# Moving weight loads and a small filter transpose within the spectral half of a transformer block

## The chip, the cores and the metric

One core of a Trainium2 chip runs the kernel. The metric is the device time of one execution in microseconds; lower is better. Several runs of each kernel are made and their median is given.

## The reference

One block with adaptive layer norm. A vector c makes six rows of 640 scales and shifts; the sequence x (2048 rows of 640, bf16) passes through a spectral filter and then through a gated feed-forward layer.

```python
mod = (silu(c) @ w_mod).reshape(1, 6, 1, -1)
sa, ca, ga, sb, cb, gb = ...                      # six rows of 640
h = layernorm(x) * (1 + ca) + sa
x = x + ga * irfft2(rfft2(h) * (w_r + 1j * w_i))  # filter over sequence and features
h = layernorm(x) * (1 + cb) + sb
x = x + gb * ((silu(h @ w_gate) * (h @ w_up)) @ w_down)
```

The feed-forward width is 1728. All inputs are bf16.

## The kernel before

The order of the work is written out by hand; no scheduler moves anything. Each engine works off its own list in program order, and waits at an instruction until what that instruction needs is there. Loads are issued by SyncE (SP) in program order as well. Eight completion counters are used in turn by the transfers, so a transfer also waits until the one eight before it has landed.

**Spectral part, forward.** Sixteen row tiles are normalised and multiplied with cosine tables (`st_a`, `st_b`, L399 to L419). The result `A_sb` lies in region `rA`. It must then be turned, feature index against time index: for most features by four transposing transfers (`t2_dma`, L537), for the rest on TensorE (`t2_pe`, L556). The filter weights are put together in region `rW` (`turn`, `wsum`).

**Spectral part, filter.** Features are worked in 21 groups of four or fewer. The loop of L770 takes group g through stages which are shifted against each other:

- `stage_a(g + 2)`: `mix` (L574) multiplies the turned features with a small table on TensorE into banks 2 and 3 or 4 and 5, and `prod` (L596) multiplies them with the filter on VectorE.
- `stage_b(g)` (L606): TensorE turns the products, ScalarE copies them. For four groups, 7, 8, 11 and 12 (`PRE`), GpSimd adds the two parts instead and a transposing transfer turns them (`presum`, L617). These are the two turning transfers, one for each pair of groups. Their results are read late, by `stage_c` at g = 14 and g = 20.
- `stage_c(u)` (L633): TensorE applies the small inverse table to two groups at a time into banks 6 and 7 (others near the end); `evac` copies that into `Em` or `Er` in region `rE`.

Into these stages are fitted: the columns of scale and shift (`mod_col`, L591, written into free columns of the bank that `mix` fills, five matmuls of one column for each of five column blocks), the ga row (`ga_mod`), and the special row, frequency zero and Nyquist, which has a small chain of its own (`sp_w`, `sp_wc`, `sp_mm`, `sp_ev`). `sp_w` turns its filter rows by eight tiny transposes into PSUM, `sp_wc` copies them to `Wsp`, and the chain ends in two small transfers into the last partition of `Em` and `Er` (L711, L712).

The block `wm_r` holds four parts of `w_mod`: 0 ga, 1 sb, 2 cb, 3 gb. Parts 0 and 1 are loaded at the start, part 2 ahead of the loop (L553), part 3 in iteration 10 (L792).

**Spectral part, inverse, and second norm.** For 16 tiles, `s1em` and `s1er` (L729, L740) multiply `Em` and `Er`, last partition included, with tables, and L1280 and L1283 finish the tile; VectorE adds the input and writes x1 (L1285). The first two tiles are normalised in iterations 3 and 4, turned by a transposing transfer (`ln2_tr(0)`, L885) and scaled and shifted on GpSimd and ScalarE (`ln2_mod`, L893, L899). The down weights are multiplied by gb on VectorE (`wd_fold`, L923), the first of them in iteration 8.

**Feed-forward part.** The first two tiles take plain products: `gu13` (L1097) for the last 64 columns, then `gu_plain` (L1109) for 13 blocks of gate and up, with silu on ScalarE and a product on VectorE (L1115, L1117), then the down product (L987). The other 14 tiles take products with fewer multiplications (L1139, L1010).

The down weights `Wd_sb` lie in region `rA`, where `A_sb` was. They are loaded after the filter loop (L828 to L833), ahead of the gate and up weights (L836 to L845):

```python
    for h in range(2):
        nc.sync.dma_start(Wd_sb[:, HK * h:HK * h + 6, :],
                          B_w_down[768 * h:768 * h + 768, :].rearrange("(fc fp) d -> fp fc d", fp=P))
    nc.sync.dma_start(Wd_sb[0:RK, 6, :], B_w_down[1536:1632, :])
    nc.sync.dma_start(Wd_sb[0:64, 13, :], B_w_down[1664:1728, :])
    nc.sync.dma_start(Wd_sb[64:RK, 13, :], B_w_down[1632:1664, :])
```

Of the kernel before, what the change touches and what calls it, by code (L numbers as in the profile page):

```python
# [11 lines left out]
BF16 = mybir.dt.bfloat16  # L12
# [6 lines left out]
NT, P = 16, 128  # L19
# [6 lines left out]
RK, HK = 96, 7  # L26
# [134 lines left out]
def _rev(ap, free_off, dims):  # L161
    a = ap[:]
    return bass.AP(tensor=a.tensor, offset=a.offset + free_off, ap=[list(a.ap[0])] + [list(d) for d in dims])
# [3 lines left out]
def adaln_block_kernel(ctx, tc, A_x, A_w_r, A_w_i, B_x, B_w_gate, B_w_up, B_w_down, c, w_mod, out):  # L167
    nc = tc.nc
# [57 lines left out]
    wm_r = rM.cut(12800, [NC5, 4, D])  # L226
# [16 lines left out]
    Wsp = rE.cut(34064, [3, 2, NT, 2], parts=81)  # L243

    psum = ctx.enter_context(tc.tile_pool(name="psum", bufs=1, space=bass.MemoryType.PSUM)).tile([P, 8, 512], F32, name="psum")

    def banks(b, n, shape=None, dt=F32):
        ap = psum[:, b:b + n, :].rearrange("p b e -> p (b e)")
        if dt == BF16:
            ap = ap.bitcast(BF16)  # L250
        if shape is not None:
            ap = ap[:, 0:int(np.prod(shape))]
            if len(shape) > 1:
                ap = ap.rearrange("p (a b) -> p a b", a=shape[0])
        return ap
# [39 lines left out]
    wm_m = wm_v[:, :, 2 * D:6 * D].rearrange("p k (i d) -> p k i d", i=4)  # L295
# [37 lines left out]
    if True:  # L333
# [87 lines left out]
        def wsum(lo, hi, rk, eng):  # L421
            for off in (lo, 161 - hi):
                v = [_rev(Wt, WP * i + 321 * rk + off, [[321, 8], [160, 2], [1, hi - lo]]) for i in range(3)]
                eng.tensor_tensor(v[1], v[2], v[0], ALU.add)  # L424
# [7 lines left out]
                                  sa4[:].unsqueeze(2).unsqueeze(3).to_broadcast([P, 4, 2, 8]))  # L432

        def sp_w():
            tp = psum[0:81, 2, 192:256].bitcast(BF16).rearrange("p (v h a k) -> p v h a k", v=2, h=2, a=2)
            for v in range(2):
                for hl in range(2):
                    for a in range(2):
                        o = 160 * (1 - a if hl else a)
                        nc.tensor.transpose(tp[:, v, hl, a], (Wrev if hl else Wrow)[:, v, o:o + 81], identb[0:16, 0:16])  # L440
            return tp

        def sp_wc(tp):
            for v in range(2):
                nc.vector.tensor_copy(Wsp[:, 2 * v].rearrange("p h k a -> p h a k"), tp[:, v])
            nc.gpsimd.tensor_tensor(Wsp[:, 1], Wsp[:, 0], Wsp[:, 2], ALU.add)

        cps = psum[:, 3, 0:NC5]
# [85 lines left out]
    if True:  # L534
# [15 lines left out]
        t2_dma(3)  # L550
        nc.sync.dma_start(Htab.rearrange("p (t h) v k -> p t h (v k)", h=2)[:, :, 0, :], H_dram.rearrange("p t v k -> p t (v k)"))
        nc.sync.dma_start(RI[:], RI_dram)
        nc.sync.dma_start(wm_r[:, :, 2, :], wm_m[:, :, 2, :])  # L553
        Wd_sb = rA.cut(0, [NFC, D])

        def t2_pe(slot):  # L556
            ls = groups[slot] + (groups[4] if slot == 3 else [])
            n = len(ls)
            tp = banks(slot % 2, 1, [8, 128], BF16)
            for i, l in enumerate(ls):  # L560
                nc.tensor.transpose(tp[:, i, :], A_sb[:, l].rearrange("p t k c r -> p (t k c r)"), identb[:])
            B2 = (rM.cut(38400 + 1024 * slot, [n, 128]) if slot < 2 else rM.cut(10240 + 1024 * (slot - 2), [n, 128]))
            if slot == 0:
                nc.scalar.copy(B2[:, 0:2], tp[:, 0:2, :])
                nc.scalar.copy(B2[:, 2:4], tp[:, 2:4, :])
            else:
                nc.scalar.copy(B2[:], tp[:, :n, :])
            spec.append((B2, 4, slice(ls[0], ls[0] + 4)))
            if n > 4:
                spec.append((B2[:, 4:6], 2, slice(0, 81, 80)))  # L570
            for i, l in enumerate(ls):
                B2of[l] = (B2, i)

        def mix(g):  # L574
            ls = groups[g]
            n = len(ls)
            xps = banks(2 + 2 * (g % 2), 2, [4, 256])
            for i, l in enumerate(ls):
                B2, j = B2of[l][0:2]
                nc.tensor.matmul(xps[:, i, 0:192], lhsT=B2[:, j, :], rhs=KS2, start=True, stop=True)  # L580
                if i == 0:
                    for c5 in {9: (0, 1, 2), 11: (3, 4), 16: (0, 1), 18: (2, 3), 20: (4,)}.get(g, ()):
                        mod_col(psum[:, 2 + 2 * (g % 2), 192 + c5:193 + c5], wm_r[:, :, 2 - g % 2], c5)
            return xps

        def stage_a(g):
            xps = mix(g)
            prod(g, xps, 0)
            prod(g, xps, 1)

        def mod_col(o, w, c5):  # L591
            for k in range(NC5):
                nc.tensor.matmul(o, lhsT=w[:, k, 128 * c5:128 * c5 + 128], rhs=sc_col[:, k:k + 1],
                                 start=(k == 0), stop=(k == NC5 - 1))
# [22 lines left out]
        def presum(g):  # L617
            b, i = PRE.index(g) // 2, 4 * (PRE.index(g) % 2)
            q = Qd[b][:, i:i + 4, :]
            P3 = PPs.pop(g).rearrange("p v h k m l -> p l (v h k m)")  # L620
            nc.gpsimd.tensor_tensor(q, P3[:, :, 0:128], P3[:, :, 64:192], ALU.add)
            Y2s[g] = Yd[b][:, i:i + 4, :]
            if i:
                nc.sync.dma_start_transpose(Yd[b], Qd[b].rearrange("p l j -> p (l j)"))
# [36 lines left out]
        def sp_gather():  # L661
            for B2, n, ls in spec:
                nc.gpsimd.tensor_tensor(B2sp[:, ls], B2[:, 0:n, 127], SA[:, ls], ALU.add)
# [102 lines left out]
        for rk in (0, 8):  # L766
            v = [_rev(Wt, WP * i + 321 * rk + 80, [[321, 8], [160, 2]]) for i in range(3)]
            nc.gpsimd.tensor_tensor(v[1], v[2], v[0], ALU.add)
        sgn_H = Htab.rearrange("p (t h) v k -> p t h (v k)", h=2)
        for g in range(NG + 1):  # L770
            if g == 9:
                nc.gpsimd.tensor_copy(sgnc[:], Kstab[:, 576:577])
            if g == 7:
                sp_gather()
            if 1 < g < NG - 2:
                if g in SPG[1:]:
                    sp_mm(SPG.index(g), g)
                if g == 2:
                    tp = sp_w()
                stage_a(g + 2)  # L780
                if g == 2:
                    wsum(32, 48, 8, nc.gpsimd)
                if g == 3:
                    sp_wc(tp)
                if g in SPG[1:]:
                    sp_ev(SPG.index(g), g)
            if g + 2 in PRE:
                presum(g + 2)
            if g in (4, 9):
                wsum(64, 80, 8 * (4, 9).index(g), nc.gpsimd)  # L790
            if g == 10:
                nc.sync.dma_start(wm_r[:, :, 3, :], wm_m[:, :, 3, :])  # L792
            if g in (11, 12):
                h4 = slice(4 * (g - 11), 4 * (g - 11) + 4)
                nc.gpsimd.tensor_scalar(sgn_H[:, h4, 1], sgn_H[:, h4, 0], sgnc[:, 0:1], 1.0, ALU.mult, ALU.mult)
            if g == 9:
                nc.vector.tensor_copy(modcols[:, 2, :], psum[:, 4, 192:197])
            if g == NG - 3:
                nc.vector.tensor_scalar_add(one_p_cb[:], psum[:, 2, 192:197], 1.0)
            if g in (14, 16):  # L800
                i = 1 - (14, 16).index(g)
                nc.gpsimd.tensor_tensor(RI[:, i], RI[:, i], ga_bc[:], ALU.mult)
            if g < NG and g not in PRE:
                Y2s[g] = stage_b(g, PPs.pop(g))
            if g == SPG[0]:
                sp_mm(0, g)
                sp_ev(0, g)
            if g == 0:
                stage_a(3)
            if g in GAG:  # L810
                ga_mod(320 * GAG.index(g), 0)
            for i in range(2):
                if TUG[i] == g:
                    turn(64, i, (g + 1) % 2, act)
            for u, gs in enumerate(units):
                if CAT[u] == g:
                    stage_c(u)
                    evac(u)
            if g == NG - 1:
                for c5 in range(NC5):  # L820
                    mod_col(psum[:, 3, 192 + c5:193 + c5], wm_r[:, :, 3], c5)
# [3 lines left out]
        s1em(1)  # L825
        gdiag = rL.cut(10496, [NC5, 128])

    for h in range(2):  # L828
        nc.sync.dma_start(Wd_sb[:, HK * h:HK * h + 6, :],
                          B_w_down[768 * h:768 * h + 768, :].rearrange("(fc fp) d -> fp fc d", fp=P))  # L830
    nc.sync.dma_start(Wd_sb[0:RK, 6, :], B_w_down[1536:1632, :])
    nc.sync.dma_start(Wd_sb[0:64, 13, :], B_w_down[1664:1728, :])
    nc.sync.dma_start(Wd_sb[64:RK, 13, :], B_w_down[1632:1664, :])  # L833
    Wgu = rW.cut(0, [2, NC5, 13 * 128])
    Wp13 = const.tile([P, NC5, 128], BF16, name="Wp13")
    nc.sync.dma_start(Wp13[:, :, 0:64], B_w_gate[:, 1664:1728].rearrange("(c5 dp) f -> dp c5 f", dp=P))  # L836
# [581 lines left out]
```

## Time and profile before

| | |
|---|---|
| three runs | 250.68, 253.23, 255.39 us (median 253.23) |
| the profiled execution | 253.03 us, of it a span of 251.3 us from the first to the last instruction |
| mean granted TensorE clock | 0.993 |
| busy share of the span | TensorE 95%, VectorE 81%, ScalarE 67%, GpSimd 31% |
| moved | 31.71 MB, 126 GB/s over the span |
| in time, about | forward to 33 us, filter to 62, inverse to 81, feed-forward from 84 |

All times inside the kernel count from the first instruction of the profiled execution. Lines such as L885 are lines of the kernel before. Engines in the profile: PE is TensorE, PEld its weight loads, DVE VectorE, ACT ScalarE, POOL GpSimd, SP SyncE; a q behind a name stands for that engine's list of issued transfers.

### The profile page before, as it was taken

How to read it: one execution, taken by the hardware profiler on the slowest of the kernel's cores; microseconds unless marked ns; L12 is line 12 of the kernel's file. 1: busy time of each engine (PE TensorE's matmuls, PEld its weight loads, DVE VectorE, ACT ScalarE, POOL GpSimd, SP SyncE). 2: the span in 40 equal slices, each digit the busy share in tenths (PEclk: the TensorE clock that was granted, in tenths of full speed). 3: DMA queues.
4: the chain of work that ended last, by engine and by line, in shares of the span. 5: the costliest groups of instructions: out<-in, count | busy, mean ns of one | idle time of the engine just before them, and what ended most of it. 6: DMA issues, size and time to landing. Idle time of an engine off the chain costs nothing.

```text
span 251.3 us, 5940 instructions
## 1 busy us (share of the span) xinstructions
PE 238.9 (95%) x2230; PEld 186.8 (74%) x2230; DVE 203.8 (81%) x479; ACT 169.3 (67%) x339; POOL 77.0 (31%) x120
## 2 busy tenths in 40 slices
PE   8789998979997899999999999999999999999994
PEld 3578888869997588778887778888765566556773
DVE  3797878967599599689999996878998788779964
ACT  4789887759987297768875387876246777774220
POOL 5368985990420805002002320000442000004410
PEclk9999999999999799999999999999999999999999
DMA  6999969896999999700002320500611000000111
GB/s 210 376 338 301 370 125 188 230 222 199 309 378 281 233 289 154 164 27 4 0 3 56 74 65 18 52 3 3 106 52 55 0 0 1 3 0 1 55 52 52
DMA packets 46254, 31.71 MB, mean 126 GB/s; under 512 B 23985, under 2 KB 43922, under 8 KB 46226
## 3 DMA queue, kind: packets, MB, share of 16 engines
q1 hardware_dynamic: 44288, 26.67, 41.2%
q0 software_dynamic: 1376, 4.26, 7.4%
q10 hardware_dynamic: 562, 0.41, 0.6%
q8 instruction: 17, 0.28, 0.5%
q14 instruction: 11, 0.09, 0.1%
HBM read 23.49 MB, written 2.62 MB: 104 GB/s over the span
## 4 chain that ended last, share of the span: by engine, by line
PE 77%; DMA 9%; DVE 4%; ACT 4%; POOL 2%; issue 2%; SPq 1%; ACTq 0%; DVEq 0%; POOLq 0%
PE psum L1139 36%; PE psum L1010 19%; PE psum L1109 6%; DMA rW<-rL 4%; DMA rM<-in_w_mod_dram 3%; PE psum L987 3%; PE psum L404 2%; DMA rX<-in_A_x_dram 2%; PE psum L733 2%; PE psum L1097 2%; DVE bn6a L337 2%; ACT rY L614 1%; PE psum L580 1%; ACT rE L407 1%; PE psum L1280 1%
## 5 line engine op out<-in xcount | busy, mean ns | idle before, releaser
L1139 PEld LDWEIGHTS <-rW 128*128 128x128 bf16 (+1 forms) x429 | 41.9, 98 | 12.6
L1139 PE MATMUL psum<-rW 128*128 128x256 bf16 (+1 forms) x247 | 42.2, 287 | 0.0
L1036 POOL TENSOR_TENSOR rM<-rM,rL 128x320 f32<-128x320 f32 x6 | 5.4, 905 | 96.6 <-ACT rL L1035 96.6
L1010 PEld LDWEIGHTS <-rE 128*128 128x128 f16 (+1 forms) x196 | 19.0, 97 | 7.8
L604 DVE TENSOR_TENSOR rM<-psum,rW 128x384 bf16<-128x384 f32 (+2 forms) x42 | 20.5, 543 | 4.5 <-PE psum L580 4.0
L1010 PE MATMUL psum<-rE 128*128 128x320 f16 (+1 forms) x147 | 22.9, 299 | 0.0
L1177 ACT COPY rX<-psum 128x384 f32<-128x384 f32 (+2 forms) x27 | 14.0, 519 | 7.3 <-PE psum L1139 7.2
L1170 ACT COPY rH<-psum 128x384 f32<-128x384 f32 (+2 forms) x27 | 13.9, 516 | 7.2 <-PE psum L1139 6.5
L1139 PEld LDWEIGHTS <-rE 128*128 128x128 f16 x156 | 15.2, 98 | 4.7
L1174 DVE TENSOR_TENSOR rH<-psum,rM 128x512 bf16<-128x512 f32 (+1 forms) x24 | 15.0, 624 | 4.1 <-PE psum L1139 2.2
L1193 ACT ACTIVATE rL<-psum 128x384 bf16<-128x384 f32 (+2 forms) x27 | 14.4, 532 | 5.4 <-PE psum L1139 3.4
L1285 DVE SCALAR_TENSOR_TENSOR rM<-psum,rX 128x640 f32<-128x640 f32 x16 | 13.1, 821 | 5.9 <-PE psum L1283 3.1
L1178 DVE TENSOR_TENSOR rX<-psum,rX 128x384 f32<-128x384 f32 (+2 forms) x27 | 16.3, 604 | 1.6 <-ACT rX L1177 1.4
L1164 ACT COPY rM<-psum 128x384 f32<-128x384 f32 (+2 forms) x27 | 13.9, 515 | 4.2 <-PE psum L1139 4.2
L1109 PE MATMUL psum<-rW 128*128 128x256 bf16 x130 | 15.8, 288 | 0.0
L1139 PE MATMUL psum<-rW,rE 128*128 128x256 bf16 (+1 forms) x78 | 15.6, 290 | 0.0
L1139 PE MATMUL psum<-rE,rY 128*128 128x256 f16 (+1 forms) x78 | 15.6, 290 | 0.0
L337 DVE BATCH_NORM_STATS2 bn6a<-rX 128x6 f32<-128x320 bf16 x30 | 13.0, 479 | 2.7 <-DMA rX<-in_A_x_dram 2.7
L1109 PEld LDWEIGHTS <-rW 128*128 128x128 bf16 x130 | 13.4, 104 | 2.2
L1194 ACT ACTIVATE rL<-rX 128x384 bf16<-128x384 f32 (+2 forms) x27 | 15.1, 558 | 0.0
L424 POOL TENSOR_TENSOR rW<-rW 128x256 bf16<-128x256 bf16 x20 | 13.6, 708 | 2.8 <-DVE rM L604 1.8
L979 DVE TENSOR_TENSOR rA<-psum,rM 128x320 bf16<-128x320 f32 (+1 forms) x27 | 12.1, 471 | 2.4 <-PE psum L987 2.3
(234 smaller groups left out, 635.1 us busy)
## 6 DMA issues: line engine op xcount, KB each, us to landing
rM<-in_w_mod_dram SPq DMA_DIRECT2D x4, 800.0 KB, 7.6
out_dram<-rA SPq DMA_DIRECT2D x31, 80.0 KB, 1.6
rX<-in_A_x_dram SPq DMA_DIRECT2D x6, 320.0 KB, 6.1
rA<-in_B_w_down_dram SPq DMA_DIRECT2D x2, 960.0 KB, 6.8
rY<-in_B_w_gate_dram POOLq DMA_DIRECT2D x2, 832.0 KB, 9.1
rW<-in_B_w_gate_dram SPq DMA_DIRECT2D x1, 1440.0 KB, 11.6
rW<-in_A_w_i_dram SPq DMA_DIRECT2D x2, 642.0 KB, 10.0
rW<-in_A_w_r_dram SPq DMA_DIRECT2D x2, 642.0 KB, 9.7
```

The lines of the kernel that those rows point to most:

```text
L337: nc.vector.bn_stats(bn6a[:, i % 2, k, :], x_sb[:, i, 320 * k:320 * k + 320])
L604: nc.vector.tensor_tensor(PPs[g][:, v0:v1, hl], xv[:, v0:v1, hl], in1, ALU.mult)
L1010: nc.tensor.matmul(o, lhsT=lhs[rows(k), k], rhs=rhs[rows(k), k], start=start and k == ks[0], stop=stop and k == ks[-1], skip_group_check=True)
L1109: nc.tensor.matmul(gu[u], lhsT=Wgu[:, u, c5, ff * 128:(ff + 1) * 128], rhs=h2T[:, :, c5, :], start=(c5 == 0), stop=(c5 == NC5 - 1))
L1139: nc.tensor.matmul(o[:, f], lhsT=w, rhs=b, start=(start and f == 0 and i == 0), stop=(stop and f == len(groups[g]) - 1 and i == len(ops) - ...
L1164: nc.scalar.copy(c0, X)
L1170: nc.scalar.copy(c2, X)
L1174: nc.vector.tensor_tensor(c11, Z, c0, ALU.add)
L1177: nc.scalar.copy(c3, X)
L1178: nc.vector.tensor_tensor(c22, Y, c3, ALU.add)
L1193: nc.scalar.activation(g21, X, ACT.Silu, scale=-1.0)
L1194: nc.scalar.activation(g22, c22, ACT.Silu, scale=-1.0)
```

## The change

Four things move; no arithmetic is added or left out.

1. The load of part 2 (cb) of `wm_r` moves from ahead of the filter loop into iteration 6, behind the first turning transfer, and the load of part 3 (gb) comes with it, from iteration 10.
2. The columns of cb, taken in groups 16, 18 and 20 before, are taken in groups 18 and 20.
3. Of the down weights, the first half (six blocks and the 96-row block 6) is loaded in iteration 10, behind the second turning transfer and ahead of the two small transfers of the special row. The second half stays after the loop.
4. The special filter rows are turned in iteration 5 instead of 2, into bank 7 instead of 2, and copied by ScalarE at once, instead of by VectorE in iteration 3.

```diff
         def sp_w():
-            tp = psum[0:81, 2, 192:256].bitcast(BF16)...
+            tp = psum[0:81, 7, 192:256].bitcast(BF16)...
 ...
         def sp_wc(tp):
             for v in range(2):
-                nc.vector.tensor_copy(Wsp[:, 2 * v].rearrange("p h k a -> p h a k"), tp[:, v])
+                nc.scalar.copy(Wsp[:, 2 * v].rearrange("p h k a -> p h a k"), tp[:, v])
 ...
-        nc.sync.dma_start(wm_r[:, :, 2, :], wm_m[:, :, 2, :])
         Wd_sb = rA.cut(0, [NFC, D])
+
+        def load_wd(h):
+            nc.sync.dma_start(Wd_sb[:, HK * h:HK * h + 6, :],
+                              B_w_down[768 * h:768 * h + 768, :].rearrange("(fc fp) d -> fp fc d", fp=P))
+            if h == 0:
+                nc.sync.dma_start(Wd_sb[0:RK, 6, :], B_w_down[1536:1632, :])
+            else:
+                nc.sync.dma_start(Wd_sb[0:64, 13, :], B_w_down[1664:1728, :])
+                nc.sync.dma_start(Wd_sb[64:RK, 13, :], B_w_down[1632:1664, :])
 ...
-                    for c5 in {9: (0, 1, 2), 11: (3, 4), 16: (0, 1), 18: (2, 3), 20: (4,)}.get(g, ()):
+                    for c5 in {9: (0, 1, 2), 11: (3, 4), 18: (0, 1, 2), 20: (3, 4)}.get(g, ()):
 ...
-                if g == 2:
-                    tp = sp_w()
                 stage_a(g + 2)
                 if g == 2:
                     wsum(32, 48, 8, nc.gpsimd)
-                if g == 3:
-                    sp_wc(tp)
+                if g == 5:
+                    sp_wc(sp_w())
 ...
+            if g == 6:
+                for i in (2, 3):
+                    nc.sync.dma_start(wm_r[:, :, i, :], wm_m[:, :, i, :])
             if g == 10:
-                nc.sync.dma_start(wm_r[:, :, 3, :], wm_m[:, :, 3, :])
+                load_wd(0)
 ...
-    for h in range(2):
-        nc.sync.dma_start(Wd_sb[:, HK * h:HK * h + 6, :], ...)
-    nc.sync.dma_start(Wd_sb[0:RK, 6, :], B_w_down[1536:1632, :])
-    nc.sync.dma_start(Wd_sb[0:64, 13, :], B_w_down[1664:1728, :])
-    nc.sync.dma_start(Wd_sb[64:RK, 13, :], B_w_down[1632:1664, :])
+    load_wd(1)
```

More of the change, by code (lines that the diff above doesn't have):

```diff
@@ L434, in sp_w @@
         def sp_w():
-            tp = psum[0:81, 2, 192:256].bitcast(BF16).rearrange("p (v h a k) -> p v h a k", v=2, h=2, a=2)
+            tp = psum[0:81, 7, 192:256].bitcast(BF16).rearrange("p (v h a k) -> p v h a k", v=2, h=2, a=2)
             for v in range(2):
@@ L826, in adaln_block_kernel @@
         gdiag = rL.cut(10496, [NC5, 128])
-    for h in range(2):
-        nc.sync.dma_start(Wd_sb[:, HK * h:HK * h + 6, :],
-                          B_w_down[768 * h:768 * h + 768, :].rearrange("(fc fp) d -> fp fc d", fp=P))
-    nc.sync.dma_start(Wd_sb[0:RK, 6, :], B_w_down[1536:1632, :])
-    nc.sync.dma_start(Wd_sb[0:64, 13, :], B_w_down[1664:1728, :])
-    nc.sync.dma_start(Wd_sb[64:RK, 13, :], B_w_down[1632:1664, :])
+    load_wd(1)
     Wgu = rW.cut(0, [2, NC5, 13 * 128])
```

## The prediction

> **What bounds the kernel now.** I read the chain that ended last first, then SyncE's queue, then TensorE and VectorE around the two places where the chain leaves the engines for a transfer, then the windows of DMA traffic.
>
> ```profile
> PE 77%; DMA 9%; DVE 4%; ACT 4%; POOL 2%; issue 2%; SPq 1%; ACTq 0%; DVEq 0%; POOLq 0%
> ```
>
> ```profile
> 37.64 0.41 PE psum L440 x8
> ...
> 40.22 0.28 DVE rE L445 x2
> ...
> 45.54 7.67 DMA rM<-in_w_mod_dram
> 53.26 0.40 PE psum L593 x10
> ...
> 61.53 0.93 ACT rE L654
> 62.50 1.29 PE psum L733 x20
> ...
> 71.69 9.34 DMA rW<-rL
> 81.13 2.20 POOL rW L893 x4
> ...
> 84.55 15.61 PE psum L1109 x130
> 100.16 7.64 PE psum L987 x56
> ...
> 109.10 24.02 PE psum L1139 x220
> ```
>
> Columns: start, length, what. From 84.55 us to the end the chain is TensorE without a break, so whatever moves the first down product (100.16) moves the end by as much. Ahead of it two transfers carry the chain. One is the load of the cb block of w_mod (scale columns), which lands at 53.21 and is read at once by ten column products. The other is the transpose of the first normalised tiles (L885): issued at 71.69, when VectorE has made its input, and landed at 81.03. GpSimd then needs 2.20 us for four scalings, and only then does the gate product start.
>
> ```profile
> 51.56 0.25 PE L580 MATMUL psum<-Ktab,rL 128*128 128x192 bf16 x1
> 53.26 0.40 PE L593 MATMUL psum<-sc_col,rM 128*128 128x1 bf16 x10 [1.45 <-DMA rM<-in_w_mod_dram]
> ...
> 55.54 0.25 PE L580 MATMUL psum<-Ktab,rM 128*128 128x192 bf16 x1
> ...
> 60.60 0.61 PE L645 MATMUL psum<-Ktab,rE 128*128 128x128 bf16 x8
> ...
> 80.06 0.30 PE L1283 MATMUL psum<-rH,rL 128*128 128x160 bf16 x2
> ```
>
> The first pause: one matmul of group 16 at 51.56, then nothing until 53.26, some 1.6 us. The second: TensorE has done its last tile at 80.36 and starts the gate product at 84.55, with about 1.1 us of work in between (five products of 0.11 and 0.55 for the last tile).
>
> ```profile
> 59.00:60.00 1.00, 1.00 (x21) 1.00 (x19) 0.62 (x3) 1.00 (x3) 0.00 (x0) 1.00 0.02 1
> 60.00:78.00 18.00, 17.82 (x279) 16.38 (x277) 13.44 (x33) 16.53 (x33) 4.72 (x8) 1.00 1.09 335
> 84.50:88.00 3.50, 3.50 (x22) 2.52 (x20) 2.43 (x7) 1.46 (x5) 2.31 (x3) 0.60 0.80 129
> ```
>
> The last three columns are granted clock, DMA share and GB/s. The DMA engines stand still around 59 and are then full until 78, at 335 GB/s, so the transpose of 71.69 joins a queue of weights. After the long pause the clock is 0.60 in 84.5 to 88.
>
> **The change part by part.** Times are the trace's; KB as the page has them.
>
> ```profile
> rM<-in_w_mod_dram SPq DMA_DIRECT2D x4, 800.0 KB, 7.6
> rA<-in_B_w_down_dram SPq DMA_DIRECT2D x2, 960.0 KB, 6.8
> rH<-tab_RI SPq DMA_DIRECT2D x1, 320.0 KB, 4.3
> ```
>
> ```profile
> 44.84 0.65 SPq L552 DMA_DIRECT2D rH<-tab_RI  x1
> ...
> 46.30 7.08 SPq L624 DMA_TRANSPOSE rE<-rE  x2
> 53.43 0.57 SPq L792 DMA_DIRECT2D rM<-in_w_mod_dram  x1
> 56.78 0.55 SPq L711 DMA_DIRECT2D rE<-rE  x1
> ...
> 58.03 1.97 SPq L829 DMA_DIRECT2D rA<-in_B_w_down_dram  x2
> ```
>
> ```profile
> L624 SPq DMA_TRANSPOSE rE<-rE x1: 1858/1858/1858, 46.3 to 46.3; - x1
> DMA to landing us min/median/max: 7.8/7.8/7.8
> ```
>
> (a) The cb load goes behind the first turning transpose and the gb load comes with it, ahead of the second. The transpose issued at 46.30 landed at 54.1, 0.9 after the cb load that stood before it. Now it stands first: RI lands at 44.84 + 4.3 = 49.1, the transpose at about 50.0, and its reader (stage C of groups 7 and 8, which ran at 54.2, just after it) is covered. The cb load follows: 800 KB at 335 GB/s are 2.4 us, while before it landed 4.1 after RI. So it lands between 52.4 and 54.1; I take 53.6, nearer to what this very load did. Its columns now sit in groups 18 and 20. Without the pause (1.6) and the ten columns in group 16 (0.3), group 18, at 55.54 before, comes at 53.6. So nothing is left of the pause, with 0 to 0.5 as its ends: up to 1.9 us gained. The 25 columns themselves stay. The gb load (issued at 53.43 before, now near 48.5) is read only after the last group and stays hidden. The second transpose now waits behind two loads: 53.6 + 2.4 + 0.9 is 57 at its landing, and its reader, at 60.60 before, comes near 59. If that cover of 2 us is gone, each us later is a us on the path.
>
> (b) The special filter rows: eight transposes (0.41 on TensorE) move from group 2 to group 5 into bank 7, and two copies leave VectorE (0.28 on the chain) for ScalarE.
>
> ```profile
> 52.27 0.29 ACT L707 CAST rE<-psum 128x41 bf16<-128x41 f32 x2 [1.21 <-DVE rM L604]
> ```
>
> ScalarE's nearest pair takes 0.29 us. Queued behind it are the group copies and the next evacuation; bank 7's next products wait for it too. Gain 0.28 at most, loss 0.41 at most if TensorE has no slack at group 5; nearest to both is zero, which I take.
>
> (c) Half of the down weights (960 + 120 KB, 1.1 MB) is issued right after the second transpose, near 53, using SyncE's time before the special output rows (56.78 before, near 55.2 now). Two issues fit: two loads of 960 KB cost 1.97. But these two small rows, without which the first inverse product (62.50) cannot start, now stand behind it in the same queue.
>
> ```profile
> L711 SPq DMA_DIRECT2D rE<-rE x1: 547/547/547, 56.8 to 56.8; - x1
> DMA to landing us min/median/max: 3.3/3.3/3.3
> ```
>
> Second transpose 57.0, plus 1.1 MB at 335 GB/s (3.3) is 60.3; the row then lands 0 to 3.3 us later. It moves 16 KB, so I take 0.7, that is 61.0. The product could start at 62.50 - 1.9 = 60.6. So of (a) 1.5 us remain: **-1.5**, ends 0 and -1.9. The Trainium skill, "DMA: Bandwidth & Descriptors", section on queues, rings and completion order, says that each DMA engine takes a ring's descriptors in order. It speaks against this change. The first transpose's landing behind the cb load agrees, and by it the row cannot land before 60.3.
>
> (d) The 1.1 MB is gone from the queue after 60: 3.3 us at 335 GB/s. The transpose of the normalised tiles is issued at 71.69 - 1.5 = 70.2. Before, it landed 3.0 after the full stretch ended (78); that stretch now ends at 74.7, so it lands at 77.7. Bounds:
>
> ```profile
> L885 SPq DMA_TRANSPOSE rW<-rM x1: 1273/1273/1273, 159.4 to 159.4; - x1
> DMA to landing us min/median/max: 4.6/4.6/4.6
> ...
> L885 SPq DMA_TRANSPOSE rW<-rL x1: 3798/3798/3798, 92.2 to 92.2; - x1
> DMA to landing us min/median/max: 9.0/9.0/9.0
> ```
>
> Alone, one took 4.6 us (74.8 here); beside other traffic, twice as large, 9.0 (79.2). From 77.7 GpSimd is done at 79.9; TensorE arrives at 80.36 - 1.5 = 78.9, works through the five products at GpSimd's pace, and after the last (0.11) and the last tile (0.55) starts the gate product at 80.6 rather than 84.55: **-2.45** beyond the -1.5. If the cover fails, each us of landing after 77.2 costs one.
>
> (e) The clock. 130 products took 15.61; 220 of the same width (109.10) took 24.02, 0.109 each, so at full clock 14.2: **-1.4**, as a pause of some 0.5 us is left where 3 were. The Trainium skill, "TensorE: Matmul & The Clock Gate", section "What's actually happening", states that about 3.4 us of idling halves the clock and that as long a busy stretch restores it. The trace agrees (0.60 above). By the page the whole loss would be about 1.7.
>
> (f) VectorE must keep up.
>
> ```profile
> 82.36 0.43 DVE L863 SCALAR_TENSOR_TENSOR rstd<-st,rstd 128x4 f32<-128x4 f32 x1
> ...
> 86.79 0.42 DVE L1115 TENSOR_TENSOR rX<-psum,rX 128x256 bf16<-128x256 f32 x1 [0.97 <-ACT rL L857]
> ...
> 100.72 0.43 DVE L1117 TENSOR_TENSOR rX<-psum,rX 32x256 bf16<-32x256 f32 x1
> ```
>
> It is free at 82.8 - 1.5 = 81.3, adds the last tile and folds (1.2), then runs what took 14.4 (86.79 to 101.15): done at 96.9, or 96.2 if its small idle times go. TensorE ends the gate products at 80.6 + 14.2 = 94.8 and needs VectorE's last piece 13 products of 0.136 later, at 96.6. Between 0 and +0.3; I take zero.
>
> Sum: -1.5 - 2.45 - 1.4 = -5.35 on the profiled execution's 253.03 (span 251.3, 1.7 around it): **247.7 us**. The three runs' median, 253.23, is 0.2 above it; they lie between 250.68 and 255.39.
>
> **The rivals.**
>
> (R1) The queue is not what holds the transpose: it still takes 9.34. For: the one at 92.2 took 9.0. Against: that one moves twice as much, and one alone took 4.6. Then only the early part stays: 251.5.
>
> (R2) The early gain is lost (cb lands late, or the rows hold the inverse product until 62.5), the late one stays. Transpose issued at 71.69, landed by 77.7, GpSimd done at 79.9, before TensorE's 80.36: gate product at 81.5 (-3.1), clock -1.4, VectorE late by some 0.7: 249.2. For: the margins in (a) and (c) are below 1 us.
>
> (R3) Slower: the two special rows, behind 1.1 MB and two loads, hold the first inverse product. Place: L733 at 62.50. Price: one us per us of landing after 62.5, and 1.4 for the clock once the pause is long. It eats the late gain of 3.8 from a landing at about 64.9 on; at 67 the time is 253.03 + 4.5 + 1.4 - 3.8 = 255.1. Against: issued at 55.2, even the transpose's 9.34 lands it at 64.5.
>
> (R4) Everything is covered: early -1.9, transpose landed at 74.8, gate product at 79.6 (-5.0 in all), clock -1.4, VectorE between 0 and +0.6: 246.6 to 247.2.
>
> **How the numbers follow.** Forecast 0.56, own range 246.8 to 248.6; R4 0.12; R2 0.14; R1 0.08; R3 0.10. The range 245.9 to 251.0 holds the forecast, R4 and R2 with the runs' scatter and leaves out R1 and R3. Two per cent (248.2 and 258.3) is about what a measurement of this kernel can tell from no change. Faster by more: some 0.45 of the forecast's 0.56, R4, and 0.03 of R2, 0.60. Slower by more: half of R3 and a little, 0.06. The rest, 0.34, is within.
>
> **What would show it.** Right: the column products no longer wait in group 16; the first inverse product starts near 61.0; the transpose lands within 7.5 us of its issue; no clock below 0.9 near 81 to 88; the first down product near 94.8. Wrong: columns of group 18 waiting past 54.1, DMA traffic pausing between 56 and 60, the inverse product waiting for a transfer past 62, or the transpose landing 9 us after its issue again.

## The result and the profile after

The changed kernel takes 250.99 us at the median of 22 runs (249.67 to 254.32), the kernel before, on the same chip, 253.32 us (22 runs, 250.68 to 256.22). The ratio is 0.9939, 95% interval 0.9911 to 0.9968: 0.6% faster, where 2.2% was forecast. (The ratios to the kernel before leave out the slow executions on both sides, so they differ a little from the quotients of the medians.) A second comparison (after_again, below) gave 0.9959 (0.9926 to 0.9992). The profiled execution took 251.63 us (span 249.8), 1.40 below the profiled one of before.

The chain that ended last, kernel after (start, length, what):

```profile
47.21 7.36 DMA rM<-in_w_mod_dram
54.62 0.53 PE psum L601 x15
...
56.11 7.38 DMA rE<-rE
63.62 1.94 PE psum L741 x20
...
74.20 6.55 DMA rW<-rL
80.86 2.50 POOL rW L897 x4
...
84.33 14.19 PE psum L1113 x130
98.52 7.64 PE psum L991 x56
```

A transfer that was not in the chain before stands in it now: `rE<-rE` at 56.11, the special row. It lands at 63.49, and only then does the first inverse product start (63.62; before 62.50). Its 20 products then take 1.94 us instead of 1.29. The transpose of the first normalised tiles is therefore issued 2.51 us later than before (74.20 against 71.69), and so lands at 80.75, almost where it landed before (81.03). The gate products start 0.22 earlier than before and run 1.42 shorter (14.19 against 15.61): that is the whole gain at the first down product, 1.64 (98.52 against 100.16).

TensorE's timeline, kernel after (the bracket is idle time and what ended it):

```profile
52.33 0.62 PE L653 MATMUL psum<-Ktab,rE 128*128 128x128 bf16 x8 [0.61 <-DMA rE<-rE]
...
54.62 0.53 PE L601 MATMUL psum<-sc_col,rM 128*128 128x1 bf16 x15 [0.70 <-DMA rM<-in_w_mod_dram]
...
61.11 0.38 PE L653 MATMUL psum<-Ktab,rY 128*128 128x128 bf16 x4
63.62 1.94 PE L741 MATMUL psum<-rH,rE 128*128 128x128 bf16 x20 [2.13 <-DMA rE<-rE]
```

Some of the pause of 1.45 us at the scale columns is left (0.70, now in group 18), 0.61 is new at the first turning transfer, and 2.13 us are new at the special row.

SyncE's issues, kernel after:

```profile
51.04 2.33 SPq L632 DMA_TRANSPOSE rE<-rE  x1
53.41 0.58 SPq L556 DMA_DIRECT2D rA<-in_B_w_down_dram  x1
54.04 1.98 SPq L559 DMA_DIRECT2D rA<-in_B_w_down_dram  x1
56.11 0.55 SPq L719 DMA_DIRECT2D rE<-rE  x1
...
60.00 0.43 SPq L840 DMA_DIRECT2D Wp<-in_B_w_gate_dram  x1
62.80 0.37 SPq L841 DMA_DIRECT2D Wp<-in_B_w_up_dram  x1
63.38 3.00 SPq L845 DMA_DIRECT2D rW<-in_B_w_gate_dram  x2
```

SyncE stands from 60.43 to 62.80. The transfer of L841 is the eighth after the first down load of L556 (53.41), so it needs that load's completion counter. So the gate loads of L845 are issued at 63.38, later than before (62.94), although 1.1 MB has left their place in the queue.

Windows of the kernel after; the last three columns are granted clock, DMA share and GB/s:

```profile
57.00:58.00 1.00, 1.00 (x25) 1.00 (x23) 1.00 (x3) 0.89 (x2) 0.00 (x0) 1.00 1.12 384
58.00:59.00 1.00, 1.00 (x21) 1.00 (x19) 0.79 (x3) 0.80 (x2) 0.00 (x0) 1.00 1.09 361
59.00:60.00 1.00, 1.00 (x22) 1.00 (x19) 0.51 (x1) 1.00 (x2) 0.00 (x0) 1.00 1.06 357
...
60.50:61.00 0.50, 0.50 (x24) 0.50 (x22) 0.46 (x2) 0.50 (x2) 0.00 (x0) 1.00 0.88 20
61.00:61.50 0.50, 0.49 (x14) 0.32 (x11) 0.50 (x2) 0.50 (x1) 0.00 (x0) 1.00 0.36 26
...
63.00:64.00 1.00, 0.38 (x7) 0.41 (x8) 0.00 (x0) 0.00 (x0) 0.00 (x0) 1.00 1.07 346
64.00:65.00 1.00, 1.00 (x14) 1.00 (x11) 0.00 (x0) 0.59 (x1) 0.00 (x0) 0.52 1.29 255
65.00:66.00 1.00, 1.00 (x13) 1.00 (x10) 0.00 (x0) 0.19 (x1) 0.00 (x0) 0.50 1.21 125
66.00:67.00 1.00, 1.00 (x8) 0.77 (x7) 0.00 (x0) 0.63 (x2) 0.00 (x0) 0.50 0.95 312
67.00:68.00 1.00, 1.00 (x15) 0.99 (x14) 0.42 (x1) 0.47 (x2) 0.00 (x0) 0.77 1.06 302
...
76.00:77.00 1.00, 1.00 (x18) 0.93 (x16) 0.73 (x3) 1.00 (x4) 0.00 (x0) 1.00 1.14 357
77.00:78.00 1.00, 1.00 (x18) 0.92 (x15) 1.00 (x4) 1.00 (x2) 0.00 (x0) 1.00 2.54 96
...
84.00:88.00 4.00, 4.00 (x40) 3.57 (x38) 3.82 (x14) 2.67 (x7) 2.85 (x4) 1.00 0.76 126
```

The clock loss has moved: none at 84 to 88 any more, but one at 64 to 67.5, behind the new pause. The full stretch of DMA traffic ends at 77, not at the forecast 74.7 (before: 78). But its end is no longer SyncE's: by the trace's packets, 0.80 of the 0.94 MB that move from 74 to 77 belong to GpSimd's list, and SyncE's last piece of weights ahead of the transpose starts at 75.4 (before: 79.2). And there is a hole at 60.5 to 61.5 (20 and 26 GB/s), two microseconds before the row lands.

### The profile page after: what moved, and what is told of

The parts are those of the page before. It is cut to its first block, busy times and chain, and to the rows that moved or that the text cites. A ratio compares the mean times of both kernels' runs of the same rounds, so it can differ in the third digit from the quotient of the medians.

```text
span 249.8 us, 5942 instructions
## 1 busy us (share of the span) xinstructions
PE 238.8 (96%) x2230; PEld 187.3 (75%) x2230; DVE 203.3 (81%) x477; ACT 169.7 (68%) x341; POOL 77.2 (31%) x120
## 4 chain that ended last, share of the span: by engine, by line
PE 75%; DMA 10%; POOL 6%; DVE 4%; ACT 1%; issue 1%; ACTq 0%; SPq 0%; DVEq 0%; POOLq 0%
PE psum L1143 36%; PE psum L1014 18%; PE psum L1113 6%; PE psum L991 3%; DMA rE<-rE 3%; DMA rM<-in_w_mod_dram 3%; DMA rW<-rL 3%; PE psum L741 2%; DMA rX<-in_A_x_dram 2%; POOL rstd L359 2%; PE psum L1101 2%; DVE bn6a L337 2%; POOL rE L371 2%; PE psum L588 1%; PE psum L619 1%
## 5 line engine op out<-in xcount | busy, mean ns | idle before, releaser
L1198 ACT ACTIVATE rL<-rX 128x384 bf16<-128x384 f32 (+2 forms) x27 | 15.1, 558 | 0.0
L745 ACT CAST rL<-psum 128x640 bf16<-128x640 f32 (+2 forms) x17 | 11.0, 659 | 5.1 <-PE psum L750 2.8
L1113 PE MATMUL psum<-rW 128*128 128x256 bf16 x130 | 14.4, 273 | 0.0
```

The costliest lines, as they stand in the source:

```text
L1113: nc.tensor.matmul(gu[u], lhsT=Wgu[:, u, c5, ff * 128:(ff + 1) * 128], rhs=h2T[:, :, c5, :], start=(c5 == 0), stop=(c5 == NC5 - 1))
L1198: nc.scalar.activation(g22, c22, ACT.Silu, scale=-1.0)
```

## The experiments

Profiled executions differ by up to 3 us in when the early part is done (the issue of the RI table, L552, lies between 43.93 and 46.96). So the table counts from that issue. "Row" and "transpose" are from issue to landing. The products' starts are those of TensorE's timeline, 0.1 to 0.2 ahead of the chain's where products overlap.

| kernel | row | first inverse product | transpose issued | transpose | gate products | first down product | end of span | clock lost |
|---|---|---|---|---|---|---|---|---|
| before | 3.3 | 17.66 | 26.85 | 9.3 | 39.50 | 55.15 | 206.46 | at the gate products |
| after | 7.4 | 18.66 | 29.24 | 6.5 | 39.21 | 53.40 | 204.84 | at the inverse products |
| row_first | 4.3 | 15.92 | 25.11 | 9.0 | 37.35 | 51.54 | 202.83 | no |
| wd_late | 3.9 | 15.86 | 25.05 | 8.5 | 36.92 | 52.78 | 204.04 | at the gate products |
| row_pool | 7.0 | 17.57 | 28.15 | 5.6 | 37.85 | 52.18 | 203.87 | at the inverse products |
| keep_warm | 6.8 | 18.14 | 27.32 | 6.4 | 37.18 | 51.37 | 202.80 | no |
| scale_only | 2.9 | 16.25 | 25.44 | 9.1 | 37.68 | 51.87 | 203.14 | no |
| wd_early_only | 5.8 | 19.09 | 28.28 | 5.9 | 37.97 | 52.30 | 203.75 | at the first columns |
| filter_rows_only | 2.3 | 19.03 | 28.21 | 8.7 | 40.33 | 54.52 | 206.02 | at the first columns |
| short_queue | 3.0 | 17.51 | 26.69 | 5.6 | 36.39 | 50.71 | 202.39 | no |
| after_short | 7.4 | 18.07 | 27.24 | 5.8 | 36.97 | 51.27 | 203.40 | no |
| row_first_short | 4.3 | 16.39 | 25.58 | 5.8 | 35.34 | 49.60 | 201.72 | no |

**The row before the weights (row_first).** From the kernel after, the first half of the down weights is issued behind the two rows:

```diff
+                if g == 15:          # behind sp_ev, which issues the two rows
+                    load_wd(0)
 ...
-            if g == 10:
-                load_wd(0)
```

> The changed kernel, with the first half of the down weights issued behind the two special output rows instead of ahead of them. Queue theory (the rows were late because 1.1 MB stood before them in SyncE's queue): the rows land 3 to 4.5 us after their issue, before 60, the first inverse product starts when ScalarE's last copy is done, at 61.5 to 62.1 instead of 63.6, the clock stays full near 64 to 67, and the time falls by 1.5 to 3 us to 248 to 249.5. Rival (the rows' own transfer, from many partitions into one, takes some 7 us in dense traffic, wherever it stands): they land past 61.5 again, the first inverse product stays at 63 or later, and the time stays within 0.7 us of the changed kernel.

Its chain:

```profile
60.09 1.29 PE psum L741 x20
...
69.28 8.98 DMA rW<-rL
78.36 2.35 POOL rW L897 x4
```

The row landed 4.3 us after its issue, the first inverse product came 2.74 earlier than in the kernel after (15.92 against 18.66 in the table) and kept its clock. The profiled execution took 248.74 us. But the transpose, now issued 4.13 earlier, takes 8.98 again and leaves a pause ahead of the gate products; in the window 78 to 82 TensorE is busy for 2.05 of 4 us. The median is 251.86 us, the ratio 0.9961 (0.9912 to 1.0009): only 3 of 10 executions had a mean clock of 0.996 or more (248.7 to 250.7 us). So the edit moves the early part as expected, and in most executions what it gains is not seen at the end.

**All down weights late (wd_late).** The same from the other side: `load_wd(0)` stands after the filter loop, ahead of `load_wd(1)`, as before.

> The changed kernel with all down weights loaded after the loop, as before; the moved scale loads and the special filter rows stay. Queue theory: the rows land before 60 and the first inverse product starts at 61.5 to 62.1, but the transpose of the first normalised tiles stands behind all the weights again, takes 8.5 us or more, and TensorE pauses ahead of the gate product and loses the clock there; time 252 to 253. Rival (the early half of the weights was of no use to that transpose): it takes 6.5 us as in the changed kernel and the time is below 251.

The first inverse product came at 15.86, as in row_first. So parts 1, 2 and 4 of the change are worth 1.8 us there (17.66 before), and it is the early down load alone that loses them. The transpose takes 8.5 us again and this execution lost its clock at the gate products, as expected; the median, 251.22, lies below the 252 to 253 that was expected. The ratio is 0.9922 (0.9865 to 0.9979).

**The rows in another queue (row_pool).** From the kernel after, both rows are issued by GpSimd:

```diff
-                nc.sync.dma_start(Em[127:128]..., Osp[:, 0:64].unsqueeze(1))
-                nc.sync.dma_start(Er[127:128]..., Osp[:, 64:80])
+                nc.gpsimd.dma_start(Em[127:128]..., Osp[:, 0:64].unsqueeze(1))
+                nc.gpsimd.dma_start(Er[127:128]..., Osp[:, 64:80])
```

> The changed kernel, with the two special output rows issued by GpSimd, whose transfers go through another ring, and all else in its place. Queue theory: they no longer stand behind the down weights, land within 4 us of about 55.5, and the first inverse product starts at 61.5 to 62.1; time 248 to 249.5. Rival (the DMA engines themselves are full, whichever ring a transfer comes by): they land at 62 or later, time within 0.7 us of the changed kernel.

GpSimd's timeline and the view of L719:

```profile
54.36 0.82 POOL L719 DMA_DIRECT2D rE<-rE  x1
55.19 0.55 POOL L720 DMA_DIRECT2D rE<-rE  x1
```

```profile
L719 POOL DMA_DIRECT2D rE<-rE x1: 822/822/822, 54.4 to 54.4; - x1
...
DMA to landing us min/median/max: 7.0/7.0/7.0
```

In a queue without the weights ahead of it the row still takes 7.0 us, as against 7.4, and 4.3 where the weights come later. So it is not the place in SyncE's list alone that delays it. (A part of the 7.0 may belong to GpSimd's own way of issuing: by the trace, the row's first piece moves 4.4 us after its issue, where GpSimd's loads at 70.11 and 80.17 need 1.5 and 1.9. No run issues the row from GpSimd without the weights.) The Trainium skill, "DMA: Bandwidth & Descriptors", section on queues, rings and completion order, has a sentence that fits: the increment that reports completion "lands only after every earlier write from that SDMA engine, across its queues". The trace agrees with it: a transfer has landed with the last of its sixteen completion steps; of the first down load fifteen steps come at 58.7 and the last at 61.15, and the row's last comes at 61.41, behind it. The kernel itself was faster, 0.9908 (0.9861 to 0.9955), at 249.19 us in the range of the queue theory, though the row was not early: the first inverse product came 1.1 sooner than in the kernel after, and the two issues no longer stand between SyncE's, so the gate loads are issued 15.1 after the table (59.04), not 18.4.

**Keep TensorE busy (keep_warm).** Nine products of 512 columns into an unused place are put ahead of the first inverse product of the kernel after (`idle_pe(9)` before `s1em(0)`); they shorten no wait.

> The changed kernel with nine dummy products of 512 columns on TensorE, written to a free bank and read by nobody, ahead of the first inverse product, some 2 us in the pause in which it waits for the special rows. If the half clock near 64 to 67 comes from that pause, the clock stays full, the first 20 inverse products take 1.3 us instead of 1.94, and the time falls by 1.0 to 1.5 us. If the clock is lowered by something else, it falls all the same and the time stays within 0.4 us.

```profile
61.30 2.11 PE L318 MATMUL psum<-ones 128*128 128x512 bf16 x9
63.24 1.28 PE L741 MATMUL psum<-rH,rE 128*128 128x128 bf16 x20
```

With work added, the first 20 products take 1.28, not 1.94, the transpose is issued at 27.32 after the table rather than 29.24, and the time is 249.95 us, ratio 0.9923 (0.9877 to 0.9968), with 9 of 10 executions at a clock of 0.996 or more. Of the kernel after it was 3 of 22, and 1 of 11 in after_again; but keep_warm and after_again ran on different chips, and on that of keep_warm the kernel before had it in 15 of 31, so the chip may have a part in it. From the first inverse product to the transpose's issue it is 9.18 us instead of 10.58: the clock lost after the new pause costs 1.4 us there. That the whole kernel gains the 1.0 to 1.5 us that was expected isn't shown: the ratio's interval overlaps that of the kernel after (0.9911 to 0.9968).

**A shorter queue ahead of the transpose (short_queue).** From the kernel *before*, without any part of the change: one gate load of 1440 KB is issued behind the transpose of the first normalised tiles instead of ahead of it.

```diff
     load_gu(0, 512, (0,))
-    load_gu(512, 1664, (0,))
     load_gu(0, 512, (1,))
 ...
                 ln2_tr(0)
+                load_gu(512, 1664, (0,))
                 load_gu(512, 1024, (1,))
```

> The kernel before, with one load moved: the second part of the gate weights (1440 KB) is issued behind the transpose of the first normalised tiles instead of ahead of it. Queue theory (that transpose took 9.34 us because weights stood before it): with 4.3 us of traffic less ahead of it, it lands within 6 us of its issue, TensorE's pause before the gate product goes and the clock stays full there; time 249.5 to 251. Rival (the transpose takes 9 us beside any traffic, also that of GpSimd's loads): it takes 8.5 to 9.5 us again, and the time stays within 0.7 us of before.

Its chain:

```profile
62.52 1.29 PE psum L733 x20
...
71.70 5.61 DMA rW<-rL
77.42 2.37 POOL rW L892 x4
79.79 10.35 DMA rY<-in_B_w_gate_dram
```

Issued at 71.70, where it was in the kernel before (71.69), the transpose takes 5.61 rather than 9.34 us. Nothing else ahead of it has changed. So the bytes queued ahead of it are what it waits for. (The last line is a load of gate weights that GpSimd issues after its scalings; in TensorE's waits no idle time stands against it.) The first down product comes 4.4 earlier (50.71 against 55.15) with the clock kept in all four runs; the ratio is 0.9848 (0.9814 to 0.9883), more than the whole change brings, though measured in another series.

**Parts of the change on the kernel before.** scale_only makes parts 1 and 2, wd_early_only part 3, filter_rows_only part 4.

> The kernel before with the moved scale loads and columns only (parts 1 and 2 of the change). If the first pause was the scale columns' alone, group 16 no longer waits, at most 0.8 us is waited for in group 18, and the first inverse product starts 1.2 to 1.8 us sooner, counted from the issue of the RI table; the special rows land in time; time 1 to 1.7 us below before. Rival (the pause only moves to group 18, and what the changed kernel gained early came from the filter rows): it starts less than 0.5 us sooner.

> The kernel before with the early half of the down weights only (part 3). Queue theory: the special rows stand behind it and land 6 to 8 us after their issue, the first inverse product starts 0.5 to 1.5 us later than before and the clock halves there; what the later transpose gains pays for it or not quite; time between 1 us below and 1 us above before. Rival (the early half is harmless by itself, the rows were late because two scale loads came late too): they land within 4.5 us and the time falls by more than 1.5 us.

> The kernel before with the moved special filter rows only (part 4). By the prediction nothing; by the changed kernel's trace the products of group 8 start some 0.5 us sooner, but that runs into the wait for the scale columns in group 16, which lasts that much longer: the first inverse product starts within 0.3 us of before, counted from the issue of the RI table, and the time is within 0.5 us.

scale_only: first inverse product 1.41 earlier than before, ratio 0.9892 (0.985 to 0.9933), the median 2.2 us below, where 1 to 1.7 was expected. wd_early_only: transpose 5.9 us, ratio 0.9917 (0.9878 to 0.9957). filter_rows_only: 1.0021 (0.9982 to 1.006), no difference that can be seen, but its first inverse product came 1.4 later in the profiled execution, where 0.3 at most was expected. Part 3 alone was expected to stay within 1 us of before; its median is 2.2 below. Parts 1 and 2 alone, and part 3 alone, thus brought no less than all four together (0.9939, 0.9959, with overlapping intervals): the gains don't add. The last two runs also showed what I had not looked for. TensorE's timeline of filter_rows_only:

```profile
54.78 0.43 PE L593 MATMUL psum<-sc_col,rM 128*128 128x1 bf16 x10 [2.03 <-DMA rM<-in_w_mod_dram]
55.07 0.64 PE L580 MATMUL psum<-Ktab,rL 128*128 128x192 bf16 x3
55.50 1.06 PE L611 MATMUL psum<-identb,rM 128*128 128x128 bf16 x8
```

After the pause for the scale columns the eight turning products take 1.06 instead of 0.61: the clock is lost there too, for some 3 us (0.50 in the windows from 55 to 58, in wd_early_only as well, there after a pause of 1.49, its row having landed at 64.11, 0.5 before the first inverse product). In the profiled execution of before, the same pause of 1.45 kept the clock. So the late first inverse products of these two kernels (19.03, 19.09) can't be read as the price of their edits.

**Both queues put right (row_first_short), and the transpose's alone (after_short).** The first is row_first with the edit of short_queue; the second is the kernel after with the edit of short_queue.

> The changed kernel with two edits: the first half of the down weights is issued behind the two special rows (iteration 15) instead of ahead of them, and one 1440 KB load of gate weights is issued behind the transpose of the first normalised tiles instead of ahead of it. Times count from the issue of the RI table. Theory (two queues, each with its own price): the rows land about 4 us after their issue, the first inverse product starts near 15.9 (18.66 in the changed kernel), the transpose lands 5 to 6.5 us after its issue (9.0 with the first edit alone), the gate product starts near 35.5 and the down product near 49.5, without loss of clock; in all some 2 us less than with the first edit alone, 246.5 to 248 us, and a median at least 3 us below the changed kernel's. Rival A (the transpose is late for a reason other than the bytes ahead of it once the start is early): its landing stays at 8.5 to 9 and the time is that of the first edit alone, 248.7 at full clock. Rival B (the gate weights issued behind it come too late): TensorE waits at the fourth or fifth gate block for weights, the down product stays near 51.5, and the time is 249 or above.

> The changed kernel with one edit: the 1440 KB load of gate weights behind the transpose of the first normalised tiles. The special rows stay behind the first half of the down weights. Theory: the transpose is already at 6.5 us in the changed kernel, of which at most 1 to 2 us can still go; the first inverse product stays near 18.7 and the clock is lost there as before, so the time falls by 0 to 1.5 us (250 to 251.5), less than the 4 us that the same edit brought the kernel before. Rival (most of the change's loss sits at the transpose after all): 247 to 248.5, as with both edits.

> The changed kernel once more, unaltered, for a comparison on the same chip with the two others. 250.5 to 251.5 us at the median and a ratio to the kernel before of 0.99 to 0.997; a ratio outside this would mean that the comparison depends on the chip.

row_first_short, chain:

```profile
61.77 1.29 PE psum L741 x20
...
79.78 0.55 PE psum L1100 x5
...
80.88 11.56 PE psum L1112 x105
...
95.62 0.76 DVE rX L1118 x2
```

No transfer stands between the inverse and the gate products any more. The transpose takes 5.8 us, and the gate products follow the last tile at 80.88 (35.34 after the table). The median is 248.35 us, the ratio to before 0.9799 (0.9754 to 0.9844), the best of all; beside the kernel after on the same chip (after_again, 251.00) the medians' ratio is 0.989. 246.5 to 248, and 3 us below the kernel after, was expected; it is 2.65. The first inverse product came 0.5 later than in row_first, and at the end of the gate products the chain goes over VectorE (L1118 at 95.62), for which TensorE waits 0.5 us. The gate weights issued behind the transpose did not hold TensorE in its waits. after_short came out at 250.96, ratio 0.9923 (0.9896 to 0.9951), the kernel after at 251.00: with the row late, shortening the second queue brings nothing that can be told apart. Its row still takes 7.37. One part of what was expected did not come: its clock was not lost. TensorE's timeline:

```profile
63.87 1.28 PE L741 MATMUL psum<-rH,rE 128*128 128x128 bf16 x20 [2.13 <-DMA rE<-rE]
```

The pause is 2.13 us, as in the kernel after, and the 20 products behind it take 1.28, not 1.94. Here too TensorE waits for VectorE at the end of the gate products (0.41 us).

## Why the prediction was wrong

Its sum, term by term, on the profiled executions (253.03 and 251.63):

| step | forecast | measured | from |
|---|---|---|---|
| (a) and (c) first inverse product | -1.5 | +1.1 | 62.50 to 63.62 |
| clock in the inverse part (not in the sum) | 0 | +1.4 | to the transpose's issue, 71.69 to 74.20, less 1.1 |
| (d) from the transpose's issue to the gate products | -2.45 | -2.7 | 12.86 to 10.13 |
| (e) the gate products' clock | -1.4 | -1.4 | 15.61 to 14.19 |
| first down product | -5.35 | -1.6 | 100.16 to 98.52 |

**(a) was nearly right.** The first turning transfer landed later than worked out (its reader waited until 52.33; 50.0 was forecast) and so did the cb load (0.70 us of waiting left). But with the down load out of the way the first inverse product gained 1.4 to 1.8 (scale_only, wd_late, row_first), around the 1.5 that the sum had.

**(c) is the step that failed.** It had the row land at 61.0: the second turning transfer at 57.0, 3.3 us of transit for the 1.1 MB, and the row 0.7 behind. The row landed at 63.49. The order was as forecast; the term of 3.3 was too small. The second turning transfer landed at 57.6, and from 57 to 60 the windows show 1.1 MB moved, as the 335 GB/s would have it. Yet the first down load was complete only 9.4 us after its issue at 53.41:

```profile
L556 SPq DMA_DIRECT2D rA<-in_B_w_down_dram x2: 582/588/595, 53.4 to 57.3; - x2
...
DMA to landing us min/median/max: 9.0/9.2/9.4
```

That is at 62.79, 5.2 us behind the turning transfer. The trace has the time of each of its sixteen completion steps: fifteen come between 60.25 and 60.33, where the forecast had them, and the last at 62.79. Of the row's steps fifteen come between 61.83 and 61.98 and the last at 63.49. Counted by the last steps the row is 0.7 behind the load, as worked out; counted by the others it is 1.6 behind, so without the late part it would have landed 1.0 past the forecast. So bytes over rate gave the time at which most of the load was there, while a transfer has landed only with its slowest part. Two things in the trace stand beside the delay. A single packet of 16 KB in the queue that the page calls "instruction" starts at 58.45 and takes 1.15 us; and in the hole, right behind 120 of the row's 128 pieces (60.0 to 60.2), pieces of weights take up to 1.1 us, where 0.06 is their median. The row's last eight pieces start at 62.6.

This was rival R3, to which I gave 0.10 with the argument that "even the transpose's 9.34 lands it at 64.5". R3's own formula, (63.49 - 62.5) + 1.4 - 3.8, gives -1.4 and 251.6 us: the measured time. It was set up as the slower case, but a landing between its two limits, 62.5 and 64.9, is a small gain, and the forecast held no case for that interval. The median, 250.99, lies at the upper end of the range, in which only rival R2 and the scatter of the runs stood: that it falls inside is luck and no support for the sum.

**The clock after a short pause** is the rest of the loss. The sum put it at nothing, and R3 counted it only "once the pause is long"; here it came behind 2.13 us (0.50 to 0.77 from 64 to 68). From the first inverse product to the transpose's issue 10.58 us pass with the loss, and 9.18 (keep_warm, which fills the pause) or 9.17 (after_short) without it. But after_short has the same pause and kept its clock, so the length of the pause alone doesn't decide it. The Trainium skill, "TensorE: Matmul & The Clock Gate", section "What's actually happening", speaks of an idle window of about 3.4 us; this row does not agree with it. Nor did the kernel before have such a window ahead of its gate products: its idle time there, some 3.1 us, is broken by five products and the last tile.

**(d): the right mechanism, and the right size partly by luck.** That the queue holds the transpose, against R1, is shown by short_queue (9.34 to 5.61). In the kernel after, SyncE's weights ahead of it ended 3.9 us earlier than before (75.4 against 79.2), near the 3.3 of the forecast, although the gate loads were issued no earlier: the counter of the down load held SyncE to 62.80. An early transfer was taken as bytes that leave the later queue; it also took a counter. But the transpose was issued 2.5 us later than before, not 1.5 earlier as in the sum, and that shortens its wait as well. In row_first, where it is issued near the forecast's time (25.11 after the table; 70.2 is 25.36), it takes 9.0, not the 7.5 that the sum had.

**(e)** was right to 0.02 us, **(b)** can't be told from zero (filter_rows_only), and **(f)** held in the kernel after; VectorE comes late, by 0.3 to 0.5 us, in the three kernels with the shorter queue (short_queue, after_short, row_first_short).

What stays open: what makes the last of the sixteen steps late. The packet of 16 KB stands near it in row_first too (55.55, 1.04 us; 120 pieces of the row by 55.7, the last eight from 56.4), but the trace doesn't name the DMA engine of a packet, so that it holds up the one engine with the last part is likely and not shown. Nor does any run show why pieces of weights slow down in the hole.

## What to carry to other kernels

A small transfer that a whole stage waits for goes ahead of the large ones in time, not only in its queue: 4.3 us against 7.4, and in GpSimd's queue it took 7.0. Before moving a load earlier, ask which short transfers then share the engines with it and whose completion counter it holds. Where a chain leaves the engines for a transfer, look first at what is queued ahead of that transfer: moving one load of 1440 KB behind it was worth more (0.985) than the four-part change (0.994), and both queues together 0.980. And a sum of bytes over rate tells when most of a transfer is there; the wait ends with its slowest part, here 2.5 us later.

## What the runs showed of the hardware

- A lost clock was one stretch of 3.4 us at a granted clock of 0.50 in each of these traces. It followed pauses of TensorE of 1.49 (wd_early_only), 1.57 (row_pool), 2.03 (filter_rows_only), 2.04 (after_again) and 2.13 us (after); pauses of 1.45 (before) and 2.13 us (after_short) kept the clock. In before and wd_late it followed the broken pause ahead of the gate products. In 15 of 31 executions of the kernel before on one chip, and 2 of 20 on another, the mean clock was 0.996 or more: the same kernel loses it in some executions and not in others.
- A row of 16 KB took 2.3 to 4.3 us where the 1.1 MB of down weights was issued behind it and 5.8 to 7.4 us where it was issued ahead, from SyncE's list and from GpSimd's (7.0).
- A transfer's sixteen completion steps can lie far apart: of the first down load fifteen came within 0.1 us and the last 2.5 us later (after); the row's last came 1.0 to 1.5 us behind the others in before and after.
- During the transpose of the normalised tiles the traffic almost stops: 96 GB/s at 77 to 78 in the kernel after, against 357 in the microsecond before. Around the second turning transfer it does not (288 GB/s from 56 to 57).
